# One score burst a step, full-size operands and fewer PSUM buffers in a top-k attention and ELU kernel

## The chip, the cores and the metric

The kernel runs on one core of a Trainium2 chip. A core has five engines with instruction streams of their own: TensorE (PE in the profile; its weight loads are PEld), VectorE (DVE), ScalarE (ACT), GpSimd (POOL) and SyncE (SP), which here only issues DMAs. They meet through semaphores. The metric is the device time of one execution in microseconds; a comparison uses the median of several.

## The reference

Eight batches, eight heads, 576 positions, head size 64, all in float32 (the feed-forward weights come as float64 words and are decoded on the chip). For each head

```python
scores = scale * np.matmul(q, k.transpose(0, 1, 3, 2))       # 576 x 576
kth = np.partition(scores, -32, axis=-1)[..., -32:-31]       # the 32nd largest of each row
scores = np.where(scores >= kth, scores, -1000000000.0)
attn = softmax(scores)
x = np.matmul(attn, v)                                        # 576 x 64
```

The heads are put side by side into 4608 rows of 512, and a feed-forward block follows: `h = x @ w_in` with 2048 columns, `g = h if h > 0 else exp(h) - 1`, `out = g @ w_out` with 512 columns.

## The kernel before

**Tiles and steps.** A row of 576 is 4 x 128 plus a remainder of 64. A *step* is one tile of 128 queries for one pair of heads; the two heads lie on partitions 0 to 63 and 64 to 127 of the transposed keys and queries (`kqT`). A *remainder step* takes the last 64 queries of four heads. There are 18 steps a batch, 144 in all. A *group* is the step or the two steps (two tiles, same pair of heads) whose attention values are computed together.

**The loop.** Iteration n works on four steps at once: scores of step n + 2 (TensorE, copied out of PSUM by ScalarE), selection of the 32 largest in step n (VectorE: eight MAX8 and six MATCH_REPLACE8, in four passes), the mask and exponential of step n - 1 (ScalarE, with two small GpSimd operations `neg` and `gap` ahead of each), its normalisation (GpSimd), and the transposes of step n - 2 (`turn`, TensorE, copied into `et` by ScalarE). When a group's last transposes are done it is put into `closing`, and the next iteration computes its values (`attend`).

**Feed-forward.** `feed` stands four times in an iteration, after each selection pass. It takes pieces from the list `ffn` by costs and due times that are fixed when the program is built: a *hidden* piece (four matmuls `hps` into one PSUM tile, two ScalarE passes into `n`, and a gate on VectorE that reads `n` and the PSUM tile) or a quarter of a *projection* (four matmuls `ops`). Gates are issued at the next `feed`. Blocks have one, two or three tiles of 128 rows, so hidden matmuls have 128, 256 or 384 columns.

**Order.** In the first 16 iterations (`n < tight`) a scheduler orders the instructions. From then on `manual_schedule` keeps TensorE, ScalarE, VectorE and GpSimd in the order of the program text, so the place of a call in the loop is its place in each engine's queue.

**The scores** (lines 280 to 299). `scores(u, half)` computes half of the 576 keys: for each head one matmul with 64 operand rows, into one two-bank PSUM tile `scps` of which there is one. It is called twice in an iteration, the first call ahead of the first pass, the second after `attend`.

**Operand shapes.** The profile gives a weight load's or matmul's rows and columns of the array as 128*128, 64*128, 128*64 or 64*64. Transposes (`eps`, `qkps`), `hps` and `ops` use 128*128; scores 64*128 (64*64 in remainder steps); values 128*64, and for the last 64 keys of each head 64*64, since the last keys' values of both heads share one chunk of `vT`, one head on each half of the partitions (lines 225 to 234, and `rows` in line 406).

**Keys and queries** (lines 236 to 265). Loaded as `kin` and `qin`, each with the last 64 positions of both heads in a fifth chunk of 64 partitions. `transpose_qk` is a generator with three pieces: four transposes of keys, four of queries, and three of 64 rows for the two remainders (keys twice, so that they lie on both sides of the queries). `turn_qk()` runs one piece, `turn_qk(True)` all that is left. It is used in four iterations a batch.

**PSUM.** Eight banks: `scps` two, three for the tag `t` (`qkps`, `eps`, `avps` in turn), three for the tag `f` (`hps`, `ops` in turn). A tile of a tag waits until the copy or gate that reads the last user of its bank is done.

Of the kernel before, what the change touches and what calls it, by code (L numbers as in the profile page):

```python
# [80 lines left out]
def kernel(  # L81
# [27 lines left out]
    def pool(name, bufs, **kw):  # L109
        return ctx.enter_context(tc.tile_pool(name=name, bufs=bufs, **kw))  # L110
# [9 lines left out]
    fpool = pool("f", 2)  # L120
    opool = pool("o", 1)
    ps_sc = pool("ps_sc", 1, space=PSUM)
    ps_t = pool("ps_t", 3, space=PSUM)
    ps_f = pool("ps_f", 3, space=PSUM)
    late = {}
    raws = ExitStack()
    early = raws.enter_context(tc.tile_pool(name="early", bufs=1))
# [81 lines left out]
    loaded, kqT, vT = {}, {}, {}  # L209

    def load_qk(b, hp):
        for name, src in (("k", k), ("q", q)):
            t = ldpool.tile([P, J + 1, 2, D], FP32, tag=name + "in", name=name + "in")
            for hh in range(2):
                nc.sync.dma_start(
                    t[:, 0:J, hh, :],
                    src[b, 2 * hp + hh, 0:JP, :].rearrange("(p j) d -> p j d", j=J),
                )
            nc.sync.dma_start(
                t[0:R, J, :, :],  # L220
                src[b, 2 * hp : 2 * hp + 2, JP:S, :].rearrange("h p d -> p h d"),
            )
            loaded[b, hp, name] = t

    def load_v(b, hp):
        t = kvpool.tile([P, 2 * J + 1, D], FP32, tag="vT", name="vT")
        for hh in range(2):
            h = 2 * hp + hh
            nc.sync.dma_start(
                t[:, hh * J : (hh + 1) * J, :],  # L230
                v[b, h, 0:JP, :].rearrange("(p j) d -> p j d", j=J),
            )
            nc.sync.dma_start(t[hh * R : (hh + 1) * R, 2 * J, :], v[b, h, JP:S, :])
        vT[b, hp] = t

    def transpose_qk(b, hp):

        d = kvpool.tile([P, 4 * J + 3, D], FP32, tag="kqT", name="kqT")
        kqT[b, hp] = d[:].rearrange("p c d -> p (c d)")
        srcs = [loaded.pop((b, hp, name)) for name in ("k", "q")]
        for i, src in enumerate(srcs):
            ps = ps_t.tile([P, JP], FP32, tag="t", name="qkps")
            for c in range(J):
                nc.tensor.transpose(  # L247
                    ps[:, c * P : (c + 1) * P],
                    src[:, c, :, :].rearrange("p h d -> p (h d)"),
                    ident[:],  # L250
                )
            c0 = KEYS + i * (2 * J + 1) * D
            nc.scalar.copy(kqT[b, hp][:, c0 : c0 + JP], ps[:])
            yield
        ps = ps_t.tile([P, JP], FP32, tag="t", name="qkps")
        for i, src in enumerate((srcs[0], *srcs)):
            nc.tensor.transpose(  # L257
                ps[:, i * R : (i + 1) * R],
                src[0:R, J, :, :].rearrange("p h d -> p (h d)"),
                ident[0:R, 0:R],  # L260
            )
        nc.scalar.copy(
            d[:, 0 : 4 * J + 3 : 2 * J + 1, :],
            ps[:, 0 : 3 * R].rearrange("p (a s) -> p a s", a=3),
        )
        yield
# [4 lines left out]
    def turn_qk(whole=False):  # L271
        while turning:
            if next(turning[0], turning) is turning:
                turning.pop(0)
            elif not whole:
                return

    turning = []

    def scores(u, half):  # L280

        if half == 0:
            u.sc = scpool.tile([P, 2, S], FP32, tag="sc", name="sc")
        ps = ps_sc.tile([P, 2, JP], FP32, tag="s", name="scps")
        q0 = QUERIES + u.t.qt * P
        for h, i, rows in u.heads:
            kq = kqT[u.t.b, h // 2]
            part = slice(i * D, (i + 1) * D)
            k0 = (KEYS if i == 0 else 0) + half * HS
            nc.tensor.matmul(  # L290
                ps[rows, i, 0:HS],
                kq[part, q0 : q0 + u.t.ql],
                kq[part, k0 : k0 + HS],
                start=True,
                stop=True,
            )
        nc.scalar.activation(  # L297
            u.sc[:, :, half * HS : (half + 1) * HS], ps[:, :, 0:HS], AF.Copy, scale=scale
        )

    def select_row(u, i):
        if i == 0:
# [72 lines left out]
    def turn(u, chunks):  # L375

        if u.turned:
            return
        g = u.group
        if g.et is None:  # L380
            g.et = etpool.tile([P, 2 * J + 1, len(g.tiles), P], FP32, tag="et", name="et")
        ps = ps_t.tile([P, JP], FP32, tag="t", name="eps")
        sc = u.sc[:, :, :].rearrange("p i s -> p (i s)")
        n = chunks.stop - chunks.start
        for c in range(n):
            c0 = (chunks.start + c) * P
            nc.tensor.transpose(ps[:, c * P : (c + 1) * P], sc[:, c0 : c0 + P], ident[:])  # L387
        nc.scalar.copy(  # L388
            g.et[:, chunks, u.at, :],
            ps[:, 0 : n * P].rearrange("p (c q) -> p c q", c=n),  # L390
        )
        if chunks.stop == 2 * J + 1:
            u.turned = True
            if u.at == len(g.tiles) - 1:
                closing.append(g)

    def attend(g):
        t = g.tiles[0]
        ps = ps_t.tile([P, JP], FP32, tag="t", name="avps")
        n = P if t.rem else sum(x.ql for x in g.tiles)  # L400
        for k in range(2 if t.rem else 1):
            hp = 2 * g.hp + k if t.rem else g.hp
            vt = vT[t.b, hp]
            for c in range(J + 1):
                for i in range(2):
                    rows = slice(0, P) if c < J else slice(i * R, (i + 1) * R)
# [14 lines left out]
        if t.rem:  # L421
            finish(t.block, 2, slice(2 * g.hp, 2 * g.hp + 2), t.cols,
                   ps[:, 0:n].rearrange("p (a q) -> p a q", a=2))
            return
        c0 = 0
        tiles = list(g.tiles)
        while tiles:
            blk, lo, parts = tiles[0].block, tiles[0].cols.start, 0
            while tiles and tiles[0].block is blk:
                parts += 1  # L430
                hi = tiles.pop(0).cols.stop
            finish(blk, parts, g.hp, slice(lo, hi), ps[:, c0 : c0 + hi - lo])
            c0 += hi - lo
# [160 lines left out]
    load_v(0, 0)  # L594
    start_qk(0, 0)
    turn_qk(True)
    scores(steps[0], 0)
    scores(steps[0], 1)
    load_qk(0, 2)
    start_qk(0, 1)  # L600
    turn_qk(True)
    scores(steps[1], 0)
    scores(steps[1], 1)
    load_qk(0, 3)
    for hp in range(1, NHP):
        load_v(0, hp)
# [9 lines left out]
    for n in range(NS + 3):  # L616
# [2 lines left out]
        ahead, cur, prev, done = step(n + 2), step(n), step(n - 1), step(n - 2)  # L619
        if n < tight:  # L620
            turn_qk(True)
            scores(ahead, 0)
            scores(ahead, 1)
            for i in range(2):
                passes = select_row(cur, i)
                next(passes)
                if i == 0:
                    while closing:
                        attend(closing.pop(0))
                elif prev:  # L630
# [13 lines left out]
            )  # L644
        passes = select(cur) if cur else iter(range(4))
        if ahead:
            scores(ahead, 0)
        next(passes)
        feed(n, 0.25)
        if prev:  # L650
            mask(prev, 0)
        turn_qk()
        while closing:
            attend(closing.pop(0))
        if ahead:
            scores(ahead, 1)
        next(passes)
        feed(n, 0.25)
        if done:
# [49 lines left out]
```

## Time and profile before

| | |
|---|---|
| median of 3 runs | 1735.36 us (1735.35 to 1737.28) |
| the profiled execution | 1733.84 us, its span 1732.0 us |
| granted TensorE clock, mean | 0.973 |
| TensorE matmuls busy | 1643.3 us, 95% of the span |
| VectorE busy | 1545.1 us, 89% |
| ScalarE busy | 1138.9 us, 66% |
| GpSimd busy | 408.0 us, 24% |
| hidden matmuls `hps` | 2304 records, 562.8 us |
| projections `ops` | 1152 records, 525.9 us |
| scores `scps` | 1280 records, 229.0 us |
| values `avps` | 2000 records, 200.5 us |
| transposes `eps` | 1296 records, 192.6 us |

A float32 matmul leaves two records in the trace, a transpose one. Matmuls are pipelined and overlap, and the records' ends are modelled, so the distance from one start to the next tells more than a record's length; matmuls on different row or column halves of the array start within some 7 ns of each other. In lines of the trace, `L290` is line 290 of the kernel, and a name such as `scps<-kqT` is the tile written and the tile read.

### The profile page before, as it was taken

How to read it: one execution, taken by the hardware profiler on the slowest of the kernel's cores; microseconds unless marked ns; L12 is line 12 of the kernel's file. 1: busy time of each engine (PE TensorE's matmuls, PEld its weight loads, DVE VectorE, ACT ScalarE, POOL GpSimd, SP SyncE). 2: the span in 40 equal slices, each digit the busy share in tenths (PEclk: the TensorE clock that was granted, in tenths of full speed). 3: DMA queues.
4: the chain of work that ended last, by engine and by line, in shares of the span. 5: the costliest groups of instructions: out<-in, count | busy, mean ns of one | idle time of the engine just before them, and what ended most of it. 6: DMA issues, size and time to landing. Idle time of an engine off the chain costs nothing.

```text
span 1732.0 us, 25403 instructions
## 1 busy us (share of the span) xinstructions
PE 1643.3 (95%) x8384; PEld 995.9 (57%) x8384; DVE 1545.1 (89%) x3376; ACT 1138.9 (66%) x2473; POOL 408.0 (24%) x1078
## 2 busy tenths in 40 slices
PE   5468899999999999999999999999999999999999
PEld 3345657475665666655556575755547475755565
DVE  6899999999999999999989998999999999998700
ACT  6786777676766766767667675757757585756521
POOL 2674222222122212222222221122222222122100
PEclk8568999999999999999999999999999999999999
DMA  6541011001100011001100011001100000000000
GB/s 164 171 137 35 21 40 36 7 12 43 48 7 7 23 39 40 1 13 42 48 13 1 27 28 54 1 13 41 39 22 1 19 23 27 7 7 7 7 12 12
DMA packets 101124, 56.17 MB, mean 32 GB/s; under 512 B 84096, under 2 KB 92288, under 8 KB 100992
## 3 DMA queue, kind: packets, MB, share of 16 engines
q1 hardware_dynamic: 100992, 54.55, 11.4%
q8 instruction: 66, 1.08, 0.3%
q14 instruction: 66, 0.54, 0.1%
HBM read 45.09 MB, written 9.44 MB: 31 GB/s over the span
## 4 chain that ended last, share of the span: by engine, by line
PE 75%; DVE 17%; ACT 1%; issue 1%; POOL 0%; ACTq 0%
PE ops L489 26%; PE hps L471 25%; PE avps L414 8%; PE scps L290 8%; PE eps L387 7%; DVE wk L334 6%; DVE m L341 6%; DVE m L329 2%; PE qkps L247 1%; DVE gT L451 1%; DVE wk L311 1%; DVE m L317 1%; ACT sc L297 0%; DVE raw L179 0%; PE qkps L257 0%
## 5 line engine op out<-in xcount | busy, mean ns | idle before, releaser
L471 PE MATMUL hps<-xT,w_in 128*128 128x256 f32 (+2 forms) x2304 | 562.8, 390 | 21.9 <-DVE gT L451 15.7
L341 DVE MAX8 m<-wk 128x8 f32<-128x576 f32 x816 | 576.8, 750 | 0.0
L489 PE MATMUL ops<-w_out,gT 128*128 128x512 f32 x1152 | 525.9, 601 | 0.0
L471 PEld LDWEIGHTS hps<-xT,w_in 128*128 128x128 f32 x2304 | 398.9, 193 | 147.5 <-DVE gT L451 26.1
L334 DVE MATCH_REPLACE8 wk<-m,wk 128x576 f32<-128x576 f32 x544 | 400.6, 746 | 0.0
L489 PEld LDWEIGHTS ops<-w_out,gT 128*128 128x128 f32 x1152 | 209.7, 191 | 238.3 <-issue 233.1
L357 ACT ACTIVATE sc<-sc,neg 128x576 f32<-128x576 f32 x288 | 224.0, 778 | 77.3 <-POOL neg L354 77.2
L367 POOL TENSOR_SCALAR dene<-den 128x2 f32<-128x2 f32 x144 | 33.2, 231 | 994.6 <-ACT sc L358 994.2
L371 POOL TENSOR_SCALAR sc<-sc,rec 128x576 f32<-128x576 f32 x288 | 214.5, 755 | 193.9 <-DVE rec L369 154.2
L290 PE MATMUL scps<-kqT 64*128 64x288 f32 (+1 forms) x1280 | 229.0, 458 | 32.7 <-ACT sc L297 23.9
L388 ACT COPY et<-eps 128x512 f32<-128x512 f32 (+1 forms) x432 | 189.4, 473 | 99.2 <-PE eps L387 99.1
L358 ACT ACTIVATE sc<-sc,gap 128x576 f32<-128x576 f32 x288 | 223.1, 775 | 26.6 <-ACT sc L357 1.9
L297 ACT ACTIVATE sc<-scps 128x576 f32<-128x576 f32 x288 | 186.0, 646 | 75.7 <-PE scps L290 70.4
L387 PE MATMUL eps<-ident,sc 128*128 128x128 f32 x1296 | 192.6, 283 | 20.4 <-POOL sc L371 17.0
L387 PEld LDWEIGHTS eps<-ident,sc 128*128 128x128 f32 x1296 | 156.4, 144 | 93.2 <-issue 49.3
L414 PE MATMUL avps<-et,vT 128*64 128x256 f32 (+5 forms) x2000 | 200.5, 335 | 4.3 <-ACT et L388 4.2
L479 ACT ACTIVATE n<-hps 128x256 f32<-128x256 f32 (+2 forms) x288 | 108.9, 378 | 141.4 <-PE hps L471 132.7
L334 DVE MATCH_REPLACE8 wk<-m,sc 128x576 f32<-128x576 f32 x272 | 200.3, 746 | 0.0
L329 DVE MAX8 m<-sc 128x8 f32<-128x576 f32 x272 | 191.7, 748 | 0.0
L451 DVE SCALAR_TENSOR_TENSOR gT<-n,hps 128x256 f32<-128x256 f32 (+2 forms) x288 | 117.2, 408 | 70.2 <-ACT n L480 69.7
L414 PEld LDWEIGHTS avps<-et,vT 128*64 128x64 f32 (+1 forms) x2000 | 113.1, 139 | 98.4 <-issue 53.2
L290 PEld LDWEIGHTS scps<-kqT 64*128 64x128 f32 (+1 forms) x1280 | 90.7, 178 | 126.2 <-issue 45.5
(40 smaller groups left out, 838.9 us busy)
## 6 DMA issues: line engine op xcount, KB each, us to landing
kin<-in_k_dram SPq DMA_DIRECT2D x64, 128.0 KB, 2.8
qin<-in_q_dram SPq DMA_DIRECT2D x64, 128.0 KB, 2.8
raw<-in_moe_w_in_dram SPq DMA_DIRECT2D x16, 512.0 KB, 4.1
vT<-in_v_dram SPq DMA_DIRECT2D x64, 128.0 KB, 2.3
raw<-in_moe_w_out_dram SPq DMA_DIRECT2D x16, 512.0 KB, 3.2
out_dram<-osb SPq DMA_DIRECT2D x32, 256.0 KB, 2.3
kin<-in_k_dram SPq DMA_DIRECT2D x32, 32.0 KB, 2.5
qin<-in_q_dram SPq DMA_DIRECT2D x32, 32.0 KB, 2.4
```

Source lines behind the costliest of these rows:

```text
L290: nc.tensor.matmul(ps[rows, i, 0:HS], kq[part, q0 : q0 + u.t.ql], kq[part, k0 : k0 + HS], start=True, stop=True,)
L329: nc.vector.max(found[i], cur[i])
L334: nc.vector.match_replace(wk[i], found[i], cur[i], TAKEN)
L341: nc.vector.max(found[i], cur[i])
L357: nc.scalar.activation(sc, sc, AF.Prelu, bias=neg[:], alpha=STEEP)
L358: nc.scalar.activation(sc, sc, AF.Exp, bias=gap[:], accum_out=u.den[:, i : i + 1])
L371: nc.gpsimd.tensor_scalar(u.sc[:, i, :], u.sc[:, i, :], rec[:, i : i + 1], 1.0, ALU.mult, ALU.mult)
L387: nc.tensor.transpose(ps[:, c * P : (c + 1) * P], sc[:, c0 : c0 + P], ident[:])
L388: nc.scalar.copy(g.et[:, chunks, u.at, :], ps[:, 0 : n * P].rearrange("p (c q) -> p c q", c=n),)
L414: nc.tensor.matmul(ps[i * D : (i + 1) * D, cols], vt[rows, 2 * J if c == J else i * J + c, :], w, start=(c == 0), stop=(c == J),)
L471: nc.tensor.matmul(ps[:, 0:n_tok], w_in[:, i, f * P : (f + 1) * P], blk.xT[:, i, 0:n_tok], start=(i == 0), stop=(i == NC - 1),)
L489: nc.tensor.matmul(blk.o[:], blk.gT[f // NG][:, f % NG, s * P : (s + 1) * P], w_out[:, f, :], start=(f == 0), stop=(f == NF - 1),)
```

## The change

- `scores` computes both halves of the keys in one call, eight records or, in remainder steps, sixteen, into one PSUM tile `wide` of four banks, which is taken once for the whole kernel. ScalarE copies it out in two operations, one for each head, as many elements as before.
- To make room, the tags `t` and `f` get two PSUM banks each instead of three. The single transpose of the middle chunk (`rest`) goes to the free end of the fourth bank of `wide` and not to a bank of `t`.
- The last queries are loaded to partitions 64 to 127 of the last chunk of `kin`, beside the last keys, and two full transposes replace the three of 64 rows.
- `vT` gets a chunk more: each head's last values have one of their own, whose other 64 partitions GpSimd fills with zeros, and the values' last matmul has 128 rows like the others.
- `attend` is called directly behind `scores`, ahead of the first pass, and the rest of `transpose_qk` directly behind the last transposes (`other`), ahead of the last pass and `feed`.

```diff
-    ps_t = pool("ps_t", 3, space=PSUM)
-    ps_f = pool("ps_f", 3, space=PSUM)
+    ps_t = pool("ps_t", 2, space=PSUM)
+    ps_f = pool("ps_f", 2, space=PSUM)
+    wide = ps_sc.tile([P, 4, JP], FP32, tag="s", name="scps")
...
             nc.sync.dma_start(
-                t[0:R, J, :, :],
+                last[0:R, J, :, :] if name == "k" else last[R:P, J, :, :],
                 src[b, 2 * hp : 2 * hp + 2, JP:S, :].rearrange("h p d -> p h d"),
             )
...
-        t = kvpool.tile([P, 2 * J + 1, D], FP32, tag="vT", name="vT")
+        t = kvpool.tile([P, 2 * J + 2, D], FP32, tag="vT", name="vT")
...
-            nc.sync.dma_start(t[hh * R : (hh + 1) * R, 2 * J, :], v[b, h, JP:S, :])
+            mine = slice(hh * R, (hh + 1) * R)
+            other = slice((1 - hh) * R, (2 - hh) * R)
+            nc.gpsimd.memset(t[other, 2 * J + hh, :], 0.0)
+            nc.sync.dma_start(t[mine, 2 * J + hh, :], v[b, h, JP:S, :])
...
-        for i, src in enumerate((srcs[0], *srcs)):
+        for i in range(2):
             nc.tensor.transpose(
-                ps[:, i * R : (i + 1) * R],
-                src[0:R, J, :, :].rearrange("p h d -> p (h d)"),
-                ident[0:R, 0:R],
+                ps[:, i * R : i * R + P],
+                srcs[0][:, J, :, :].rearrange("p h d -> p (h d)"),
+                ident[:],
             )
...
-    def scores(u, half):
+    def scores(u):
...
+        for half in range(2):
+            for h, i, rows in u.heads:
+                kq = kqT[u.t.b, h // 2]
+                part = slice(i * D, (i + 1) * D)
+                k0 = (KEYS if i == 0 else 0) + half * HS
+                nc.tensor.matmul(
+                    wide[rows, 2 * i + half, 0:HS],
+                    kq[part, q0 : q0 + u.t.ql],
+                    kq[part, k0 : k0 + HS],
+                    start=True,
+                    stop=True,
+                )
+        for i in range(2):
+            nc.scalar.activation(
+                u.sc[:, i, :].rearrange("p (a s) -> p a s", a=2),
+                wide[:, 2 * i : 2 * i + 2, 0:HS], AF.Copy, scale=scale,
             )
...
-        ps = ps_t.tile([P, JP], FP32, tag="t", name="eps")
+        if chunks.stop - chunks.start == 1:
+            ps = wide[:, 3, HS : HS + P]
+        else:
+            ps = ps_t.tile([P, JP], FP32, tag="t", name="eps")
...
-                    w = g.et[rows, chunk, :, :].rearrange("p a q -> p (a q)")
+                    w = g.et[:, chunk, :, :].rearrange("p a q -> p (a q)")
...
-                        vt[rows, 2 * J if c == J else i * J + c, :],
+                        vt[:, 2 * J + i if c == J else i * J + c, :],
...
         if ahead:
-            scores(ahead, 0)
+            scores(ahead)
+        while closing:
+            attend(closing.pop(0))
         next(passes)
         feed(n, 0.25)
         if prev:
             mask(prev, 0)
         turn_qk()
-        while closing:
-            attend(closing.pop(0))
-        if ahead:
-            scores(ahead, 1)
         next(passes)
         feed(n, 0.25)
...
         if done:
             turn(done, other)
+        turn_qk(True)
         next(passes)
         if prev:
             normalise(prev)
         feed(n, 0.25)
-        turn_qk(True)
```

The calls ahead of the loop and in its first 16 iterations change alike: `scores(x)` once for `scores(x, 0)` and `scores(x, 1)`.

More of the change, by code (lines that the diff above doesn't have):

```diff
@@ L212, in load_qk @@
         for name, src in (("k", k), ("q", q)):
-            t = ldpool.tile([P, J + 1, 2, D], FP32, tag=name + "in", name=name + "in")
+            n = J + 1 if name == "k" else J
+            t = ldpool.tile([P, n, 2, D], FP32, tag=name + "in", name=name + "in")
+            if name == "k":
+                last = t
             for hh in range(2):
@@ L278 @@
     turning = []
-    def scores(u, half):
-        if half == 0:
-            u.sc = scpool.tile([P, 2, S], FP32, tag="sc", name="sc")
-        ps = ps_sc.tile([P, 2, JP], FP32, tag="s", name="scps")
+    def scores(u):
+        u.sc = scpool.tile([P, 2, S], FP32, tag="sc", name="sc")
         q0 = QUERIES + u.t.qt * P
[L286 to L295, printed above, removed]
-            )
-        nc.scalar.activation(
-            u.sc[:, :, half * HS : (half + 1) * HS], ps[:, :, 0:HS], AF.Copy, scale=scale
-        )
+        for half in range(2):
[14 more added lines that the diff above has]
+                wide[:, 2 * i : 2 * i + 2, 0:HS], AF.Copy, scale=scale,
+            )
     def select_row(u, i):
@@ L405, in attend @@
                 for i in range(2):
-                    rows = slice(0, P) if c < J else slice(i * R, (i + 1) * R)
                     chunk = J if c == J else i * (J + 1) + c
-                    w = g.et[rows, chunk, :, :].rearrange("p a q -> p (a q)")
+                    w = g.et[:, chunk, :, :].rearrange("p a q -> p (a q)")
                     cols = slice(0, n)
@@ L596 @@
     turn_qk(True)
-    scores(steps[0], 0)
-    scores(steps[0], 1)
+    scores(steps[0])
     load_qk(0, 2)
@@ L601 @@
     turn_qk(True)
-    scores(steps[1], 0)
-    scores(steps[1], 1)
+    scores(steps[1])
     load_qk(0, 3)
@@ L646 @@
         if ahead:
-            scores(ahead, 0)
+            scores(ahead)
+        while closing:
+            attend(closing.pop(0))
         next(passes)
@@ L652 @@
         turn_qk()
-        while closing:
-            attend(closing.pop(0))
-        if ahead:
-            scores(ahead, 1)
         next(passes)
```

## The prediction

> **What bounds the kernel now.** I read the page first, then busy time by stretch, the waits from 430 us on, and TensorE's and ScalarE's order of time.
>
> ```profile
> PE 1643.3 (95%) x8384; PEld 995.9 (57%) x8384; DVE 1545.1 (89%) x3376; ACT 1138.9 (66%) x2473; POOL 408.0 (24%) x1078
> ```
>
> TensorE and VectorE are both nearly full. The next view gives length of the stretch, then the busy time of PE, PEld, DVE, ACT and POOL.
>
> ```profile
> 220.00:430.00 210.00, 205.67 (x1131) 126.06 (x1132) 210.00 (x466) 146.74 (x323) 46.99 (x140) 0.99 0.11 29
> 430.00:700.00 270.00, 267.98 (x1462) 169.96 (x1461) 257.43 (x576) 187.62 (x422) 58.76 (x175) 1.00 0.10 27
> 1300.00:1560.00 260.00, 258.50 (x1365) 161.12 (x1363) 242.83 (x536) 176.17 (x386) 55.12 (x164) 1.00 0.05 14
> ```
>
> To 430 us VectorE never stops (210.00 of 210); a faster TensorE gains nothing there. After that TensorE has no gaps. VectorE idles 65.7 us between 430 and 1560 (1130 less the busy 1064.3 of the stretches), and its waits say for whom: gates whose matmul and ScalarE pass are late.
>
> ```profile
> DVE gT L451 <- ACT n L480: 69.4, 44, 24.5
> PE scps L290 <- ACT sc L297: 6.3, 10, 0.8
> ```
>
> So from loop iteration n = 36 (432 us) TensorE's sequence is the time, with VectorE 6% under it. After 1637 us only TensorE's feed-forward work is left. Now TensorE's order of time (start, length with tail, group):
>
> ```profile
> 819.98 2.75 PE L471 MATMUL hps<-xT,w_in 128*128 128x384 f32 x8
> 822.56 0.60 PE L387 MATMUL eps<-ident,sc 128*128 128x128 f32 x4
> 823.00 2.75 PE L471 MATMUL hps<-xT,w_in 128*128 128x384 f32 x8
> ...
> 829.43 0.76 PE L290 MATMUL scps<-kqT 64*128 64x288 f32 x4
> 830.12 2.85 PE L471 MATMUL hps<-xT,w_in 128*128 128x384 f32 x8
> 832.80 0.71 PE L387 MATMUL eps<-ident,sc 128*128 128x128 f32 x5
> ...
> 836.78 0.60 PE L387 MATMUL eps<-ident,sc 128*128 128x128 f32 x4
> 837.31 0.76 PE L290 MATMUL scps<-kqT 64*128 64x288 f32 x4
> 838.00 3.70 PE L489 MATMUL ops<-w_out,gT 128*128 128x512 f32 x8
> ```
>
> Read start to start. Four transposes before full-size work last 0.44 (822.56 to 823.00), before a score burst 0.53: a change of operand shape costs 0.09. Eight hidden matmuls after full-size work last 2.58 (819.98 to 822.56), after a score burst 2.68: the new run's second weight load is late, another 0.10. A score burst is two pairs of 288 columns; at 0.216 per 256 columns (hidden runs) that is 0.49, and it lasts 0.69: 0.10 late load, 0.09 change out. A burst thus costs 0.39 us beyond its work.
>
> [...]
>
> **The change, part by part.**
>
> *Shapes.* A step without attention values has two bursts, so four changes; now two: 2 x 0.09 + 0.10 + 0.10 = 0.39 less. A step with values has six (score in and out, values in, their 64-row last chunk, second burst, out) and now three: 3 x 0.09, and 0.25 of late loads instead of 0.50, so 0.52 less. In a remainder step the last chunk comes twice, more again. Laying these intervals on the instruction order of both programs from n = 36 gives 545 changes before, 279 after, and 1294.4 us of TensorE work against 1251.5: 42.9 less. On before the same sum falls 5 us short of the 1299.5 that the trace has there, which is its waits. Padding is free: columns set the time, and they don't change.
>
> *Keys and queries.* Three 64-row transposes become two full ones (0.22). Before they mostly stand beside a score burst and add 0.17 to it. Nothing to gain, 28 x 0.05 lost; it is in the sum.
>
> *One burst in four banks.* Before, the second burst waited for ScalarE's copy of the first when nothing lay between: the wait above and single gaps of 0.9 in seven iterations, 6.5 us from 430 us on. These go.
>
> *VectorE as floor.* In stretches of four iterations I set TensorE's new sum against VectorE's busy time. In some (from n = 36, 40, 44, 60, 80, 96, 116, 132, 136) VectorE is larger, by 0.7 to 2.7; together 11.7 us of the gain is not to be had.
>
> *Two buffers instead of three.* For the transposes this hits one place. In the iterations that turn the next keys and queries, the last query piece now follows at once on the second transposes (eps, four) and the q transposes. With two buffers, the next tile (last keys and queries, new line 266) takes the buffer of those second transposes, so TensorE waits for ScalarE to copy them. ScalarE is behind:
>
> ```profile
> 622.95 0.73 ACT L388 COPY et<-eps 128x512 f32<-128x512 f32 x2
> 623.58 0.79 ACT L357 ACTIVATE sc<-sc,neg 128x576 f32<-128x576 f32 x1
> 624.46 0.78 ACT L358 ACTIVATE sc<-sc,gap 128x576 f32<-128x576 f32 x1
> 625.14 0.19 ACT L358 ACTIVATION_READ_ACCUMULATOR sc<-sc,gap 128x1 f32 x1
> 625.23 0.36 ACT L479 ACTIVATE n<-hps 128x256 f32<-128x256 f32 x1
> 625.62 0.42 ACT L480 ACTIVATE n<-n 128x256 f32<-128x256 f32 x1
> 625.95 0.57 ACT L388 COPY et<-eps 128x512 f32<-128x512 f32 x1
> ```
>
> The second transposes began at 623.97; their copy ends at 626.52. TensorE would be at line 266 after 0.44 + 0.44, at 624.85: 1.7 us of standing still, with the feed-forward matmuls, the next scores and their ScalarE passes queued behind. For the twenty such iterations from n = 49 the same subtraction on the trace gives 0.4 (projection stretches) to 2.6, mean 1.6. One copy of 0.65 (second half's scores) leaves ScalarE's order ahead of this point for the step's start, so I take 1.35: 27 us. Ends: 0.4 (18 saved of the 27) and 2.1. Twelve earlier ones fall where VectorE is the bound: nothing.
>
> For the hidden layers two buffers make a matmul wait for the gate two back. In before's trace a hidden matmul would have started ahead of that gate's end some two times per 100 us, 0.5 to 1 us each, from 500 us on (13 us in all, some where VectorE is the bound): 5, between 0 and 12.
>
> *Order and helpers.* Values directly behind scores need the second transposes' copy: TensorE gets there 1.8 us or more after those began, the copies end after 1.2 in projection stretches, and elsewhere a hidden matmul (1.7) lies between: nothing, 5 us if that cover were gone. 64 fills of 64x64 on GpSimd, nearest row its 128x128 fill of 0.20 us: 13 us on an engine 24% busy; behind them stand neg and gap, for which ScalarE waits. At most four together, 0.8 us, after the normalisation when GpSimd idles: nothing, at most 5. The loads keep their number (last queries land in the key tile), their wait for the buffer and a lead of two iterations on the sync queue. The first 16 steps are reordered by a scheduler: 0, give or take 5. Small waits of two nearly equal engines on each other: 1.5.
>
> **Sum.** 42.9 + 6.5 - 11.7 = 37.7 us possible; less 27, 5 and 1.5: 4.2 us faster. The profiled execution took 1733.8 (span 1732.0 and 1.8 around it): 1729.6; the median shown is 1.5 above it, so 1731.
>
> **Rivals.**
> *The wait for the second buffer decides it against the change.* Following one hidden step by hand in the new order with the durations above, ScalarE is 0.9 behind when the first transposes end (score copies, prelu and exp, key copy), then 0.6 + 1.65 + 0.8 + 0.5 until the second copy is done, against TensorE's 2.4: 2.1 us. Twenty of these are 42: 37.7 - 42 - 5 - 1.5, so 11 us slower, 1746. It turns at a mean wait of 1.56 us. For it: before's own mean of 1.6. Against it: waits for hidden gates just ahead would overlap with it.
> *The waits are hidden and VectorE becomes the bound.* If ScalarE, with less TensorE work between its inputs, is done in time (0.4 each, 8 us): 37.7 - 8 - 2 = 28 faster, 1707. For it: projection stretches show 0.4. Against it: four of five batches' hidden iterations show 1.7 and more.
> *The savings turn into idle time of TensorE*, because VectorE paces more of it than stretches of four show: no change, 1735; it lies inside the forecast's own range.
>
> **Chances.** Forecast 0.45, own range 1718 to 1742; slower rival 0.35; VectorE-bound rival 0.20. Measurement can tell about 0.2%, 3.5 us. Of the forecast 0.27 is faster by more, 0.13 within, 0.05 slower: faster 0.47, same 0.13, slower 0.40. The range runs from just under the fast rival, 1703, to the slow one with gate waits at 12 and fills at 5: 1756.
>
> **What would show it.** Right: score bursts of eight at about 1.17 from start to next start, no 64-row values; PE waits at line 266 for ScalarE's et copy, 28 times, 1 to 2.5 us in hidden stretches; VectorE idle from 430 to 1560 still near 50. Wrong: line 266 waits near nothing (then VectorE is gapless after 430), or waits of hidden matmuls for gates above 15 us, or VectorE's first 430 us longer than before.

## The result and the profile after

The changed kernel takes 1778.82 us (median of 4 runs, 1776.67 to 1780.35) against 1735.69 for the kernel before on the same chip: a ratio of 1.0248, 95% interval 1.0235 to 1.0261. It is 43 us slower, outside the range of the prediction and on the side of its slower rival, but four times as far as that rival went (43 for 11). The profiled execution has a span of 1778.6 us (before: 1732.0), so the traces below differ by 46.6 us where the medians differ by 43.1.

One thing to set right above: `tight` is twice the four pairs of heads, 8, so the scheduler orders the first 8 iterations, not the first 16. No number depends on it.

The page of the changed kernel, busy time by engine:

```profile
PE 1620.2 (91%) x8352; PEld 1024.8 (58%) x8352; DVE 1548.4 (87%) x3376; ACT 1141.0 (64%) x2473; POOL 416.8 (23%) x1142
```

Every engine's work is about what it was, and TensorE's is smaller; the span grew. So the loss is mostly waiting. The same stretches as before (length, then busy time of PE, PEld, DVE, ACT, POOL, then the granted clock):

```profile
220.00:430.00 210.00, 193.65 (x1106) 127.01 (x1106) 200.53 (x446) 142.30 (x315) 47.75 (x146) 0.96 0.09 24
430.00:700.00 270.00, 252.90 (x1355) 161.98 (x1352) 244.27 (x546) 175.78 (x393) 56.85 (x180) 0.99 0.11 29
1300.00:1560.00 260.00, 250.12 (x1303) 160.66 (x1302) 235.22 (x519) 171.92 (x375) 55.52 (x171) 1.00 0.06 16
```

Before, PE had 205.67, 267.98 and 258.50 here and DVE 210.00, 257.43 and 242.83. Now both have gaps in the same stretches, the first one included, where VectorE had none at all. Over the four stretches from 430 to 1560 VectorE is idle for 94.6 us (1130 less 1035.4 busy), where it was 65.7 and where the prediction wanted "near 50". Who waits for whom, from 430 to 1560 us (us in total, times, longest):

```profile
DVE gT L463 <- ACT n L492: 46.3, 38, 3.5
PEld hps L483 <- DVE gT L463: 40.0, 59, 3.1
PEld qkps L266 <- ACT et L401: 35.8, 22, 2.7
PE qkps L266 <- ACT et L401: 30.6, 22, 2.5
PE hps L483 <- DVE gT L463: 20.4, 27, 2.8
```

In the kernel before the same view has these:

```profile
DVE rec L369 <- POOL dene L367: 49.4, 33, 2.8
DVE gT L451 <- ACT n L480: 16.2, 22, 1.7
PE hps L471 <- DVE gT L451: 0.5, 1, 0.5
```

The first is VectorE's reciprocal of the softmax sums, which waits for GpSimd's step on them; it has 47.8 us in the changed kernel. So what VectorE's idle time gained, it gained at the gates.

Two waits of TensorE are new. Line 266 (last keys and queries) waits for ScalarE's copy out of the buffer that the second transposes used: this one was foreseen. A hidden matmul `hps` waits for VectorE's gate, and VectorE's gate waits for ScalarE's passes over an earlier hidden tile: three engines, each waiting for the next. The first kind, in TensorE's order of time (start, length with tail, group):

```profile
624.80 1.99 PE L483 MATMUL hps<-xT,w_in 128*128 128x256 f32 x8
626.63 0.60 PE L400 MATMUL eps<-ident,sc 128*128 128x128 f32 x4
627.07 0.60 PE L256 MATMUL qkps<-ident,qin 128*128 128x128 f32 x4
629.25 0.44 PE L266 MATMUL qkps<-ident,kin 128*128 128x128 f32 x2 [1.59 <-ACT et L401]
629.53 1.89 PE L483 MATMUL hps<-xT,w_in 128*128 128x256 f32 x8
631.35 1.24 PE L298 MATMUL scps<-kqT 64*128 64x288 f32 x8
632.52 2.38 PE L426 MATMUL avps<-et,vT 128*64 128x256 f32 x20
634.83 3.72 PE L483 MATMUL hps<-xT,w_in 128*128 128x256 f32 x16
```

and ScalarE at that point:

```profile
626.26 0.79 ACT L367 ACTIVATE sc<-sc,neg 128x576 f32<-128x576 f32 x1
627.14 0.78 ACT L368 ACTIVATE sc<-sc,gap 128x576 f32<-128x576 f32 x1
627.83 0.18 ACT L368 ACTIVATION_READ_ACCUMULATOR sc<-sc,gap 128x1 f32 x1
627.92 0.36 ACT L491 ACTIVATE n<-hps 128x256 f32<-128x256 f32 x1
628.31 0.42 ACT L492 ACTIVATE n<-n 128x256 f32<-128x256 f32 x1
628.63 0.57 ACT L401 COPY et<-eps 128x512 f32<-128x512 f32 x1
```

The second transposes start at 626.63 and could be copied at 627.2; ScalarE reaches the copy at 628.63, behind a mask and a hidden tile, and line 266 starts when it ends. The second kind is visible one step later. Scores and values run from 631.35 to 634.83, 3.48 us in one piece, and only then comes the first hidden piece of the iteration. VectorE's gate after the second selection pass wants just that piece:

```profile
634.12 1.41 DVE L351 MAX8 m<-wk 128x8 f32<-128x576 f32 x2
637.73 0.42 DVE L463 SCALAR_TENSOR_TENSOR gT<-n,hps 128x256 f32<-128x256 f32 x1 [2.19 <-ACT n L492]
```

Now the account. A matmul is counted as late when it starts more than 0.11 us (0.20 at a change of shape) later than the work of the one before it takes: 0.216 per 256 columns, 0.11 for a transpose, as in undisturbed runs of the trace. TensorE's time lost so, in us:

| | 0 to 220 | 220 to 430 | 430 to 1560 | of the last: `hps` | line 266 | scores |
|---|---|---|---|---|---|---|
| before | 95.3 | 10.5 | 8.6 | 0.7 | 0 | 7.9 |
| after | 106.2 | 28.4 | 73.8 | 32.6 | 34.2 | 0.2 |

From the start of iteration 36 (VectorE's first MAX8 of that step: 431.1 us before, 448.1 after) to the end, the trace has 1300.9 us before and 1330.5 after. The prediction's 1251.5 us of TensorE work plus 73.8, plus 2.4 lost after 1560, is 1327.7. The work was computed rightly to within 3 us; the waits were not. VectorE's step starts say when it is lost: 4.5 us by iteration 8, 6.1 by 16, 17.0 by 36, 46.2 by 138, and 46.7 at the last MAX8. After that both kernels need 95 us.

Not all that is late is a wait. Between 220 and 430 us the trace of the changed kernel has five stretches of 3.4 us in which the granted clock is one half, and four more up to 1560; the kernel before has one and none. In these stretches a matmul starts 0.427 us after one of 256 columns and 0.853 after one of 512, where the rest of the trace has 0.216 and 0.429. The account counts the difference as late: 7.8 of the 28.4 us and 6.6 of the 73.8 (3.7 and 3.2 of them under `hps`), against 1.7 and nothing before. It is no chance of one execution: the four of the changed kernel have a mean granted clock of 0.964 to 0.968, all of the kernel before that stand beside the experiments 0.971 to 0.976. Each of the nine stretches begins during a TensorE wait of 1.6 us or more or within 1 us after it, six of them at line 266. Whether they follow from the waits, no run here tests.

### The profile page after: what moved, and what is told of

The parts are those of the page before. It is cut to its first block, busy times and chain, and to the rows that moved or that the text cites. A ratio compares the mean times of both kernels' runs of the same rounds, so it can differ in the third digit from the quotient of the medians.

```text
span 1778.6 us, 25703 instructions
## 1 busy us (share of the span) xinstructions
PE 1620.2 (91%) x8352; PEld 1024.8 (58%) x8352; DVE 1548.4 (87%) x3376; ACT 1141.0 (64%) x2473; POOL 416.8 (23%) x1142
## 4 chain that ended last, share of the span: by engine, by line
PE 58%; DVE 25%; ACT 10%; issue 3%; POOL 1%; DMA 0%; ACTq 0%; POOLq 0%
PE ops L501 24%; PE hps L483 15%; DVE wk L344 10%; DVE m L351 8%; PE avps L426 8%; PE scps L298 6%; PE eps L400 3%; DVE m L339 3%; ACT sc L367 2%; DVE gT L463 2%; ACT et L401 2%; ACT sc L368 2%; ACT n L492 2%; ACT n L491 1%; PE qkps L266 1%
## 5 line engine op out<-in xcount | busy, mean ns | idle before, releaser
L483 PEld LDWEIGHTS hps<-xT,w_in 128*128 128x128 f32 x2304 | 406.3, 195 | 191.8 <-DVE gT L463 74.2
L306 ACT ACTIVATE sc<-scps 128x576 f32<-128x576 f32 x288 | 171.8, 646 | 118.6 <-PE scps L298 117.5
L401 ACT COPY et<-eps 128x512 f32<-128x512 f32 x288 | 164.8, 572 | 89.0 <-PE eps L400 89.0
L400 PEld LDWEIGHTS eps<-ident,sc 128*128 128x128 f32 x1152 | 145.7, 145 | 88.0 <-issue 48.9
L400 PE MATMUL eps<-ident,sc 128*128 128x128 f32 x1152 | 177.8, 281 | 19.9 <-POOL sc L381 18.7
L298 PE MATMUL scps<-kqT 64*128 64x288 f32 (+1 forms) x1280 | 187.9, 438 | 0.8 <-ACT et L401 0.7
L426 PE MATMUL avps<-et,vT 128*64 128x256 f32 (+2 forms) x2000 | 185.2, 330 | 2.7 <-ACT et L401 2.5
L426 PEld LDWEIGHTS avps<-et,vT 128*64 128x64 f32 x2000 | 115.5, 140 | 74.5 <-issue 27.8
L298 PEld LDWEIGHTS scps<-kqT 64*128 64x128 f32 (+1 forms) x1280 | 101.9, 181 | 75.9 <-issue 38.3
```

What stands on the lines that cost most here:

```text
L298: nc.tensor.matmul(wide[rows, 2 * i + half, 0:HS], kq[part, q0 : q0 + u.t.ql], kq[part, k0 : k0 + HS], start=True, stop=True,)
L401: nc.scalar.copy(g.et[:, chunks, u.at, :], ps[:, 0 : n * P].rearrange("p (c q) -> p c q", c=n),)
L426: nc.tensor.matmul(ps[i * D : (i + 1) * D, cols], vt[:, 2 * J + i if c == J else i * J + c, :], w, start=(c == 0), stop=(c == J),)
L483: nc.tensor.matmul(ps[:, 0:n_tok], w_in[:, i, f * P : (f + 1) * P], blk.xT[:, i, 0:n_tok], start=(i == 0), stop=(i == NC - 1),)
```

## The experiments

Two theories: the loss is **the wait at line 266**, or it is **the gates**, and then either because the hidden layers have two buffers or because the values now stand ahead of the hidden pieces. The differences below are between medians, to runs of the kernel before on the same chip (after: +43.1). A plus in a diff is what the experiment has in place of the minus.

### Values at their old place (e1_values_late)

```diff
 (after)
         if ahead:
             scores(ahead)
-        while closing:
-            attend(closing.pop(0))
         next(passes)
...
         turn_qk()
+        while closing:
+            attend(closing.pop(0))
         next(passes)
```

> The changed kernel with the values back at their old place, behind the key transposes and ahead of the second pass. Order theory (values right behind the scores put 3.5 us of TensorE work ahead of the iteration's first hidden piece, so VectorE stands at that piece's gate, and TensorE two pieces later at VectorE): hidden waits for gates from 430 to 1560 us fall from 32.6 to about 15 us and the time to 1750 to 1760. Buffer theory (two banks for hidden and projection tiles are enough to cause the gate waits): they stay above 28 us and the time stays within 6 us of 1779.

1754.48 us, ratio 1.0117 [1.0102, 1.0132]: +19.2, so 24 us under the changed kernel, as the order theory had it. The waits from 430 to 1560:

```profile
DVE gT L463 <- ACT n L492: 34.7, 36, 3.3
PE qkps L266 <- ACT et L401: 31.9, 22, 2.5
PE hps L483 <- DVE gT L463: 9.3, 10, 2.1
```

The late `hps` fall from 32.6 to 14.6 us by the account's measure (27 to 10 entries in this view), the wait at line 266 stays. The place of the values alone is worth 24 us of the 43, and the prediction had it at nothing. This is the net: with the values away from the scores TensorE has 319 changes of operand shape from iteration 36 on instead of 277, some 6 us by the prediction's prices (an estimate, 42 x 0.14: 0.09 for the change, 0.05 for the load behind it). And it includes the clock: what is late at half clock from 220 to 1560 falls from 14.4 to 8.3 us.

### A buffer of its own for the last keys and queries (e2_last_spare)

```diff
 (after)
-        ps = ps_t.tile([P, JP], FP32, tag="t", name="qkps")
+        ps = wide[:, 0, HS : HS + 3 * R]
         for i in range(2):
```

> The changed kernel with the last keys' and queries' two transposes (line 266) written to the free end of the first score bank, so that they take no bank of the transposes' two. Key-wait theory (the 34 us at line 266 from 430 to 1560 us lie on the path): the waits there go to below 3 us and the time falls by 25 to 40, to 1739 to 1754. Rival (VectorE and the gates set the pace, a wait at line 266 only takes the place of a gate wait): the time falls by less than 15, and waits for gates grow by most of the rest.

1744.07 us, ratio 1.0049 [1.0033, 1.0066]: +8.8, so 34 us under the changed kernel (35 between the bare medians, which come from two chips). The free end of the first score bank takes the tile, and line 266 is never late from 430 us on (34.2 before the edit). The gates are as they were:

```profile
PE hps L483 <- DVE gT L463: 21.1, 28, 2.8
```

The scores now lose 11.2 us, since a new burst waits until ScalarE has copied the free end of that bank out. The 22 waits with 34.2 us, and 8.4 more ahead of 430, were worth 34 us of time although the 11.2 came in their place: a wait at this point comes through to the end, and what is late at half clock falls from 14.4 to 9.3 us.

### Two buffers for the hidden layers, nothing else (e3_before_f2)

```diff
 (before)
-    ps_f = pool("ps_f", 3, space=PSUM)
+    ps_f = pool("ps_f", 2, space=PSUM)
```

> The kernel before with two banks instead of three for hidden and projection tiles, nothing else. Buffer theory: TensorE waits for gates for 25 us or more from 430 us on, and VectorE is late before 430 us too: 1755 to 1775 in all, slower by 20 to 40. Order theory: with the old order two banks do little, hidden waits of 5 to 13 us, 1738 to 1748.

1754.14 us, ratio 1.0111 [1.0096, 1.0126]: +18.9. It lies between the two expectations, nearer to the buffer theory in time and at the edge of the order theory's waits. From 430 to 1560:

```profile
PEld hps L471 <- DVE gT L451: 24.5, 40, 1.5
DVE gT L451 <- ACT n L480: 23.0, 36, 1.7
PE hps L471 <- DVE gT L451: 9.3, 16, 1.3
```

The account has 13.2 us of late `hps` there (0.7 before), and the stretch from iteration 36 to 138 takes 1141.5 us instead of 1127.8, 13.7 more: the wait is the loss, nearly one for one. Another 6.0 us are lost by iteration 36, in the stretch where VectorE had been without a gap.

### Values directly behind scores, nothing else (e4_before_values_early)

```diff
 (before)
         if ahead:
             scores(ahead, 0)
+        while closing:
+            attend(closing.pop(0))
         next(passes)
...
         turn_qk()
-        while closing:
-            attend(closing.pop(0))
```

> The kernel before with three banks each and one move: the values stand right behind the first score burst, ahead of the first pass. Order theory: VectorE waits for the first gate of each iteration with values, 1 to 2 us in some 50 of them, and where VectorE has no slack the time goes up: 1745 to 1765. Buffer theory: with three banks the move costs nothing, 1733 to 1740.

1745.61 us, ratio 1.0059 [1.0044, 1.0074]: +10.4, just inside what the order theory had. TensorE hardly waits for gates (1.8 us), as it has three buffers. VectorE waits longer at a time (3.6 and 2.2 us, where 1.7 was the longest), but not in some 50 iterations, and hardly longer in sum (16.2 us before):

```profile
DVE gT L451 <- ACT n L480: 17.4, 22, 3.6
```

Of the loss 4.5 us stand at iteration 36 (1.8 of them at iteration 8, ahead of which the edit changes nothing) and 4.7 more come by 138. TensorE's late time there grows by 2.4 us only. So the order costs about 10 us with three buffers too, but through which wait is traced for a small part of it; in the changed kernel, with two, taking it back was worth 24.

### Both together on the kernel before (e7_before_early_f2)

The edits of e3_before_f2 and e4_before_values_early in one kernel.

> The kernel before with two banks for hidden and projection tiles and the values right behind the first score burst, both at once (each alone cost 19 and 10). If the two make the loop in which VectorE waits for the first hidden piece and TensorE two pieces later for its gate, they cost more than their sum: 1769 or more, and waits for gates over 25 us from 430 to 1560. If they only add up: 1760 to 1767, with gate waits of about 15.

1769.05 us, ratio 1.0199 [1.0184, 1.0214]: +34.1, where the two alone add up to 29.3. Late `hps` come to 19.4 us (13.2 and 1.8 alone, 0.7 before), under the 25 that was expected of a loop:

```profile
DVE gT L451 <- ACT n L480: 27.7, 37, 3.6
PE hps L471 <- DVE gT L451: 14.0, 22, 1.4
```

Buffers and order make each other worse, by some 5 us in time and in late `hps` alike. The 5 us of time are little more than the three intervals leave open (2.6 us each). In the changed kernel the same gate costs more (32.6 us late), and the difference isn't settled.

### The free part of the change alone (e5_before_padded)

The kernel before with the zeros and the joint turning, and nothing else: buffers, score bursts and order stay.

```diff
 (before)
-                t[0:R, J, :, :],
+                last[0:R, J, :, :] if name == "k" else last[R:P, J, :, :],
...
-            nc.sync.dma_start(t[hh * R : (hh + 1) * R, 2 * J, :], v[b, h, JP:S, :])
+            nc.gpsimd.memset(t[other, 2 * J + hh, :], 0.0)
+            nc.sync.dma_start(t[mine, 2 * J + hh, :], v[b, h, JP:S, :])
...
-        for i, src in enumerate((srcs[0], *srcs)):
+        for i in range(2):
             nc.tensor.transpose(
-                ps[:, i * R : (i + 1) * R],
-                src[0:R, J, :, :].rearrange("p h d -> p (h d)"),
-                ident[0:R, 0:R],
+                ps[:, i * R : i * R + P],
+                srcs[0][:, J, :, :].rearrange("p h d -> p (h d)"),
+                ident[:],
...
-                        vt[rows, 2 * J if c == J else i * J + c, :],
+                        vt[:, 2 * J + i if c == J else i * J + c, :],
```

> The kernel before with the operand shapes alone: last values padded with zeros, last keys and queries turned together; order, half bursts and three banks each as before. Pricing a shape change at 0.09 us and the late load behind it at 0.05 to 0.10, TensorE has 9.9 us less to do from iteration 36 on, and no new wait: 1725 to 1729. If removed changes only turn into idle time of TensorE: 1733 to 1737.

1722.14 us, ratio 0.993 [0.9915, 0.9945]: 12.8 us *faster* than the kernel before, more than expected, and the shortest time of the study (its interval overlaps those of e6_both and e9_mid_gate below). From iteration 36 on it has 462 changes of operand shape instead of 545, for which the prediction's prices give 9.9 us less TensorE work; iterations 36 to 138 take 1117.4 us instead of 1127.8, 10.4 less, and 36 to the end 11.4 less. From 430 to 1560:

```profile
DVE gT L456 <- ACT n L485: 14.8, 22, 1.7
PE hps L476 <- DVE gT L456: 0.6, 1, 0.6
```

No wait was added, and the saving arrives whole. The price of a shape change, which the prediction took from the trace, is about right for these 83 changes.

### Both cures on the changed kernel (e6_both)

The edits of e1_values_late and e2_last_spare in one kernel.

> The changed kernel with the two changes of e1 and e2 together: values at their old place, and line 266 written to the free end of a score bank. If the two waits are separate, their gains add (24 and 35): 1715 to 1725, faster than before by 10 to 20. If they cover the same time, the second brings less than half: 1733 to 1744.

1725.93 us, ratio 0.9952 [0.9937, 0.9967]: 9.0 us faster than before and 52 under the changed kernel, where 24 and 34 add up to 58: the gains add but for 6 us. With these two waits gone the change is a gain. It doesn't beat e5_before_padded, though it has less TensorE work. By the prediction's prices the changed kernel has 33 us less (42.9 less 9.9), and the values at their old place take some 6 of that back, as in e1_values_late; iterations 36 to 138 without what is late say 25 (1084.0 for 1108.7). The waits:

```profile
DVE gT L463 <- ACT n L492: 17.6, 25, 1.7
PE scps L298 <- ACT kqT L271: 11.1, 15, 1.3
PE hps L483 <- DVE gT L463: 9.3, 10, 2.1
```

TensorE still loses 31.2 us from 430 to 1560 (13.7 gates, 13.6 scores waiting for the key copy out of their bank), against 8.7 in e5_before_padded, and its iteration 36 starts 5.2 us later. Iterations 36 to 138 are 2.2 us shorter (1115.2 for 1117.4): 22.5 of the 25 go to what is left of the waits, and 5.2 are lost ahead of them. VectorE idles 53.3 us from 430 to 1560, so it isn't the bound by itself either.

### Two transpose buffers alone (e8_before_t2)

```diff
 (before)
-    ps_t = pool("ps_t", 3, space=PSUM)
+    ps_t = pool("ps_t", 2, space=PSUM)
```

> The kernel before with two banks instead of three for transposes and values, nothing else. If the wait at line 266 comes from two banks and the new place of the last turns together, two banks in the old order cost little: 1735 to 1742. If two banks alone are to blame: 1755 or more.

1790.97 us, ratio 1.0327 [1.031, 1.0344]: +56.0, more than the whole change. Two banks alone are to blame then, in the old order too. Where the second transposes of a step (`other`) follow at once on `main` and `rest`, they wait for ScalarE's copy two tiles back; from 430 to 1560:

```profile
PE eps L387 <- ACT et L388: 21.2, 30, 1.1
PE qkps L257 <- ACT et L388: 3.6, 7, 0.9
```

By the account late `eps` come to 31.5 us. The changed kernel has none of these: there the middle chunk's transpose (`rest`) goes to the score tile and takes no buffer of this tag. That part of the change, which the prediction didn't price, seems to be what makes two buffers bearable (no run takes it alone out of the changed kernel), and the one place left without such a refuge was line 266.

### More places for gates (e9_mid_gate)

VectorE takes a ready gate also between the replacements and the searches of a pass, so that a buffer can come free half a pass earlier.

```diff
 (e6_both)
                 nc.vector.match_replace(wk[i], found[i], cur[i], TAKEN)
+            close_gates()
             cur = wk
```

> e6 with the waiting gates issued also in the middle of each selection pass, between its replacements and its searches, so that a gate stands 1.4 us earlier in VectorE's queue. If the two hidden banks cost what they do because a gate stands behind a whole pass of 2.9 us: TensorE's waits for gates fall below 7 us from 430 to 1560 and the time to 1712 to 1720. If gates are not ready that early (ScalarE is late), VectorE waits in its place: VectorE's waits for ScalarE's n grow from 18 to 40 us or more, and the time is 1728 to 1750.

1725.63 us, ratio 0.9945 [0.993, 0.9959]: as e6_both. TensorE's wait is a little shorter, VectorE's two and a half times as long:

```profile
DVE gT L464 <- ACT n L493: 44.1, 27, 4.0
PE hps L484 <- DVE gT L464: 7.5, 15, 2.1
```

Of the two expectations the first missed (7.5 us for under 7, and no gain); of the second the wait came and its loss of time didn't. The gates can't be taken earlier because ScalarE's passes aren't done, and VectorE stands at them for longer than TensorE is spared.

### Three hidden buffers with the one burst (e10_three_f)

With four banks for scores, a third hidden buffer leaves one for transposes. Keys and queries are then turned in the free ends of the four score banks, the last keys and queries in the single bank together with the keys, and `turn_qk` goes ahead of `mask`; its call behind the last transposes is gone.

```diff
 (e6_both)
-    ps_t = pool("ps_t", 2, space=PSUM)
-    ps_f = pool("ps_f", 2, space=PSUM)
+    ps_t = pool("ps_t", 1, space=PSUM)
+    ps_f = pool("ps_f", 3, space=PSUM)
...
-                    ps[:, c * P : (c + 1) * P],
+                    wide[:, c, HS : HS + P],
...
+        turn_qk()
         if prev:
             mask(prev, 0)
-        turn_qk()
```

> e6 with three banks for hidden and projection tiles and one for the rest: keys and queries are turned in the free ends of the four score banks, keys with the last piece in one iteration, queries in the next, both ahead of the mask. If the third bank for hidden tiles is worth what its loss cost the kernel before (19 us) and one bank for transposes and values costs less than 8: 1708 to 1718, the fastest of all. If the single bank makes the second transposes wait for the copy of the first (waits of transposes for ScalarE above 25 us from 430 to 1560): 1730 to 1760.

1783.30 us, ratio 1.0278 [1.0261, 1.0295]: +48.3.

```profile
PE eps L402 <- ACT et L403: 21.9, 31, 1.5
PE scps L255 <- ACT sc L308: 20.9, 17, 1.3
```

The gate waits are gone (1.4 us), and 47.6 us of transposes and 23.6 us of keys stand in their place. Of the eight banks that the kernel before takes, one burst of four leaves four. This split of them, with the order that it was run in, is worse than two and two.

### Last keys and queries right behind the keys (e11_last_first)

To end the scores' wait for the key copy in e6_both, the last tile is turned one call earlier, in the iteration of the keys.

```diff
 (e6_both)
             nc.scalar.copy(kqT[b, hp][:, c0 : c0 + JP], ps[:])
+            if i == 0:
+                ps = wide[:, 0, HS : HS + 3 * R]
...
             yield
-        ps = wide[:, 0, HS : HS + 3 * R]
```

> e6 with the last keys and queries turned (still in the free end of the first score bank) right after the keys, a good half iteration earlier, so that their copy is done long before the next scores want that bank; in e6 TensorE waits 11 us at the scores for it from 430 to 1560. If TensorE is still what sets the pace there: 1712 to 1720, faster than the padded kernel of e5 (1722). If VectorE and the gates set it by now: 1722 to 1728, and the waits go over to hidden matmuls.

1734.03 us (median of 12), ratio 0.9994 [0.9985, 1.0003]: no different from the kernel before, 8 slower than e6_both, and both expectations missed. The scores no longer wait, but the middle chunk's transpose does, and for the same copy:

```profile
PE scps L400 <- ACT kqT L271: 12.0, 14, 2.5
```

Late are now 14.3 us of these and 5.2 us at line 266, where 13.6 us of scores were late. That is 6 us in sum; the other 2 of the 8 are not traced. The transpose writes the fourth bank of `wide` and the copy reads the first: they share the tile and no data. So these waits come with putting everything into one tile; whether they go with separate tiles was not tried.

## Why the prediction was wrong

**Right.** The price of a shape change and of the late weight load, nearly: TensorE's work with the waits comes to 1327.7 for 1330.5, a score burst takes 1.17 us from start to start (631.35 to 632.52), and e5_before_padded turned 9.9 us of computed work into 11.4 of time. In the trace of before, from 430 us on, a hidden matmul of 256 columns is followed after 0.216 us, and after 0.309 where the next one has another operand shape (a transpose: 0.109 and 0.203); behind such a change the second matmul of a hidden run starts 0.320 us after the first (a second transpose 0.165). What the account leaves of the trace after iteration 36 falls from 1292.3 to 1254.3, so 38.0 us of work were saved and not 42.9. Padding cost nothing: pairs of value matmuls of 256 columns start 0.22 us apart with 128 rows in the trace of before, and 0.27 with 64; with 128 rows the next start comes after 0.109 us for 128 columns (a transpose), 0.216 for 256, 0.323 for 384 and 0.429 for 512. The wait of the second score burst is gone (7.9 to 0.2). The wait at line 266 has the place, the cause and nearly the size foreseen: 22 waits of 1.55 us mean, 34.2 us by the account (30.6 of TensorE idle in the view), where 27 was taken from 20 of 1.35; e2_last_spare made it 34 us of time. The slower rival had 42 for it. The fills cost less than thought, 64 of 0.148 us. Of the signs that the prediction named for being wrong, two are what happened: hidden gate waits above 15 us, and a longer first 430 us.

**"Values directly behind scores ... nothing, 5 us if that cover were gone."** This is the step that failed most: a cost put at nothing. It asked only whether the values' input, the copy of the second transposes, is there in time, and that it is (values lost 0.2 us). It didn't ask who stands behind the values. At 632.52 they hold up the first hidden piece by 2.31 us, ScalarE's passes with it, and VectorE stands at the gate of just this piece after the second pass. Measured: 10 us in the old kernel, where this wait explains a small part, and 24 in the new (e4_before_values_early, e1_values_late).

**"For the hidden layers two buffers ... 5, between 0 and 12."** The trace of before had given 13 us of matmuls that would start ahead of the gate two back, from 500 us on. e3_before_f2 has 9.2 late from 500 to 1560 and 13.2 from 430. The reading was near; cutting it to 5, on the ground that part falls where VectorE is the bound, was the error, and so was leaving out what lies ahead of 430: the two banks cost 13.7 us from iteration 36 to 138 and 6.0 before it, 18.9 in all. In the changed kernel `hps` are 32.6 us late, and 14.6 with the values put back. The two terms were priced one by one, each in the old order; in e7_before_early_f2 they come to some 5 us more than their sum, which is at the edge of what the intervals can tell.

**"Twelve earlier ones fall where VectorE is the bound: nothing."** VectorE without a gap from 220 to 430 was read as cover for TensorE. But TensorE had 205.67 of 210 there. With both engines full neither had room for a wait of the other: line 266 lost 8.4 us there, `hps` 7.8, and iteration 36 starts 17.0 us late. The half clock has 7.8 us of late starts in this stretch (1.7 before), which the prediction didn't think of. Of the 17.0, 10.0 go when the values are put back and 7.7 when line 266 has its own place (438.1 and 440.4 for 448.1).

**"... its waits say for whom: gates ..."** The line shown for this counts to the end of the kernel. From 430 to 1560, where the 65.7 us stand, VectorE waited 16.2 us at gates and 49.4 for the sums of the softmax. No term of the sum was taken from it, but it hid that little of VectorE's idle time had been spent at gates before, and that the change would add 30 us there.

**The sum.** Foreseen were 37.7 possible and 33.5 given back. What TensorE was late by from iteration 36 on is 76.2 less the 8.6 that were there before, 67.6 (6.6 of it at half clock); the work saved is 42.9 as computed, 38.0 by the account. With the latter that makes the 29.6 us that iteration 36 to the end took longer; 17.0 came ahead of it.

**The rivals.** The slower rival, 1746, had the right mechanism and half the cause. Its point of decision (a mean of 1.56 us at line 266) was almost exactly met, 1.55 by the account, so by this term the kernel would have come out about even. The gates, and the first 430 us, decided it. The VectorE-bound rival is refuted: VectorE's idle time from 430 to 1560 grew from 65.7 to 94.6.

**Open.** How much of the 24 us in e1_values_late is order and how much the interplay with two buffers (e7_before_early_f2 gives some 5 for the interplay in the old kernel); most of the 10 us of e4_before_values_early; whether the lower clock comes from the waits; 2 of the 8 us of e11_last_first; and whether one burst in four banks can be had without the remaining waits of e6_both. The fastest of the kernels is the one without it.

## What to carry to other kernels

Price a moved block by what stands behind it: on its own engine the next instructions start later by its length (here 2.31 us), and one looks up which engine, kept in program order, waits for the first of them (here VectorE at its gate, for 2.19 us). Before a buffer is given up, count in the trace how often its next user would have come ahead of its last reader, and take that count whole, in stretches too where another engine seems to be the bound: where two engines were both nearly full here (205.67 and 210.00 of 210 us), neither covered a wait of the other. When a change has a part that takes no buffer and moves nothing, run that part alone first: here it was a gain of 12.8 us in a change that lost 43. And look at the granted clock beside the waits: of the 102.2 us by which TensorE was late here from 220 to 1560, 14.4 were matmuls at half clock.

## What the runs showed that was not expected

- Giving up one of three transpose buffers costs 56.0 us (e8_before_t2), one of three hidden buffers 18.9 (e3_before_f2), with TensorE's work unchanged.
- VectorE, given its gates earlier in its order (e9_mid_gate), waited 44.1 us at them instead of 17.6, with selection work behind them that needed none of it, and the time stayed within 0.3 us (1725.63 for 1725.93).
- A GpSimd fill of 64x64 took 148 ns, one of 128x128 204 ns: a quarter of the elements takes seven tenths of the time.
